# Two small loads on GpSimd's queue, tiles ahead of a weight, no zero products, and a new table of ranks in a gated spectral and dense mix

## The chip, the cores and the metric

The kernel runs on one core of a Trainium2 chip. Its engines each run a program of their own in order: TensorE (PE) multiplies, VectorE (DVE) and ScalarE (ACT) work element by element, GpSimd (POOL) and SyncE (SP) here mostly issue DMAs; ACT issues three. The metric is the device time of one execution in microseconds, and less is better. Times come from several runs; the profile comes from one further, recorded execution.

## The reference, cut to what matters

```python
def reference(A_x, A_w_r, A_w_i, B_x, B_w1, B_b1, B_w2, B_b2, gate_w):   # x: 1 x 2048 x 512
    x = A_x
    g = sigmoid((x * gate_w).sum(-1, keepdims=True))
    a = irfft2(rfft2(x) * (A_w_r + 1j * A_w_i))          # weights 2048 x 257
    b = gelu(x @ B_w1 + B_b1) @ B_w2 + B_b2              # 512 -> 1792 -> 512
    return g * a + (1 - g) * b
```

The input x is A_x in both branches. All is float32.

## The kernel before, in words

The 2048 tokens are 16 tiles j of 128; tile j of x has its 512 features on partitions, in four quarters. Tile class c is j mod 4, so class 0 holds the tiles 0, 4, 8, 12. A product in full precision is made of three products in a faster format (fp32r): each operand is split into a high part (h, by ACT) and a low part (l, by DVE: the rest), and hh, hl and lh are summed in PSUM. So `mxh`, `mxl` are the parts of x, `wa0h`, `wa0l` those of the first block of B_w1 (14 blocks f of 128 columns), `wb0h`, `wb0l` of B_w2, `g0_6h`, `g0_6l` those of the gelu output of class 0, block 6.

The spectral branch goes through `forward` for each tile (sums and differences of the quarters `eo` and `w`, a transform over the features into `pd`, one over the tokens of the tile into `py`, result `y`), then radix-4 steps between tiles on DVE (`stage1`, `filt`, `stage4`, tiles named a0, b1, c0 and so on; `filt` multiplies by the filter `wf`), then `inverse` (`pz`, `pa`). The gate's weights (`gw`, in the tile `g3`) are combined by five tiny DVE operations and put as two columns into the constant `cf` of the feature transform, so that the logits fall out of `pd`.

The dense branch has two halves. For the classes 0 and 1, `mlp` makes for each block f a group `ph` of 12 products of 512 columns, ACT applies bias (`b1t`) and gelu, the result is split, and `down` sums groups `po` over the blocks. The first group, class 0 and block 0, starts tile by tile: its products have 128 or 256 columns, since only tiles 0 and 4 are there at first. For the classes 2 and 3, `fast` makes two blocks of weights against two classes of tokens with seven products instead of eight: it uses sums of inputs (`xf11`, `xft1` and so on), of weights (`wa0h0`, `wash0`, `wath0`), two groups `nu` and two banks `ux0`, `ux1` that live through the whole half. A bank of `ux` receives by an ACT copy a result already made, and products are then added on top without the flag that starts a group. Before the first use both banks are set by one product each with a zero tile (`zerob`, lines 1168 to 1171).

PSUM has eight banks in two groups; of the class `ph` at most two are open, so a third group `ph` waits until the low part of the one two before has been read out by DVE.

What sets the order: the code adds about 2000 steps to a graph, each with an engine, a cost and a lag, and what it reads and writes. The table `RANKS` holds one number for each step, in the order in which the code adds them; a low number goes first. `schedule` plays the engines with costs and lags and takes on each engine the ready step with the lowest rank; that gives each engine's order, which is fixed at run time. A queue's DMAs are issued in that order too, each as soon as its semaphore and its tile are free. On the chip an engine that waits holds up all behind it.

The lines that the steps touch: x tiles are loaded by `load_x` (line 569); tiles 0 (by ACT's queue) and 4 by lines 594 and 596; gate weights by line 600; `cf` by 602; the bias by 625; weights by `load_w` (981 for block 0, 984 for others, 968 for those that a copy makes negative). POOL issues the DMAs that add while they write (line 498), and clears some columns of `zb` at the start (607).

## Time and profile before

| | us |
|---|---|
| median of 3 runs (365.37 to 367.65) | 365.63 |
| the profiled execution | 368.04 |
| its span, first to last instruction | 366.2 |
| PE busy | 358.7 |
| DVE busy | 327.8 |
| ACT busy | 256.7 |
| POOL busy | 69.6 |

The profiled execution's time lies 1.84 us above its span. In a row of the timeline stand start, duration, engine, line, operation, output and inputs, how many in a row, and in brackets the idle time ahead of it with what ended it. PE rows overlap: a product's duration is longer than the distance to the next. In a row of the waits stand who waited for whom, then the sum in us, the number of times and the longest. In a row of the DMA view, the last number is the median from issue to landing. In a row of the windows, behind the stretch and its length, stand the busy times of PE, of its weight loads, of DVE, ACT and POOL, then the granted clock, the share of the DMA engines and GB/s. A digit of the page's second part is a tenth of busy time.

### The profile page before, as it was taken

Reading aid. Unit: us, or ns where it says so; the run is one execution under the profiler, and the core shown is the slowest. Engines: PE = TensorE matmul, PEld = TensorE weight load, DVE = VectorE, ACT = ScalarE, POOL = GpSimd, SP = SyncE. Lnnn points to the kernel's source line nnn. Section 1 sums busy time; section 2 is a strip of 40 time slices with the busy share of each in tenths; the row PEclk is TensorE's granted clock in tenths of the full one; section 3 lists DMA queues with packets and bytes.
Section 4 is the critical chain, followed back from the end, with each engine's and each line's share of the span. In section 5 each row is a group of like instructions: output and inputs, shape, how many; then the busy total and the mean of one; then the engine's idle time right before and its main releaser. Section 6 shows DMA issues by size and latency. Waiting matters only on the chain.

```text
span 366.2 us, 5746 instructions
## 1 busy us (share of the span) xinstructions
PE 358.7 (98%) x1808; PEld 302.9 (83%) x1808; DVE 327.8 (90%) x746; ACT 256.7 (70%) x471; POOL 69.6 (19%) x89
## 2 busy tenths in 40 slices
PE   8999999999999999999999999999999999999994
PEld 8888898898878778878888788888888888888884
DVE  5999988998759999899999999999999769899962
ACT  4985778789986241753759975999999998655200
POOL 0210001100211311410333100002333112121220
PEclk9999999999999999999999999999999999999999
DMA  7999785647885937999999943339887637799896
GB/s 224 306 322 303 253 233 166 106 149 233 206 204 129 189 58 155 273 263 365 196 153 217 264 85 117 86 122 225 126 141 150 100 64 156 173 296 241 199 250 184
DMA packets 46719, 70.35 MB, mean 192 GB/s; under 512 B 5600, under 2 KB 19424, under 8 KB 46688
## 3 DMA queue, kind: packets, MB, share of 16 engines
q1 hardware_dynamic: 34880, 48.93, 41.8%
q0 software_dynamic: 11376, 20.71, 35.3%
q10 hardware_dynamic: 432, 0.33, 0.3%
q8 instruction: 14, 0.23, 0.3%
q14 instruction: 17, 0.14, 0.1%
HBM read 48.32 MB, written 19.41 MB: 185 GB/s over the span
## 4 chain that ended last, share of the span: by engine, by line
PE 75%; DVE 12%; DMA 5%; ACT 4%; issue 2%; SPq 1%; DVEq 0%; ACTq 0%
PE poB L507 20%; PE po L507 13%; PE ph L507 11%; PE ux L1185 9%; PE nu L1185 7%; PE pd L507 4%; PE pz L507 3%; PE py L507 3%; PE pa L507 3%; DVE m L856 3%; DMA wf<-in_wf 3%; DMA y<-ownr 1%; DMA xf<-in_xt 1%; DVE y L760 1%; DVE y L758 1%
## 5 line engine op out<-in xcount | busy, mean ns | idle before, releaser
L995 ACT ACTIVATE ph<-ph,b1t 128x512 f32<-128x512 f32 x28 | 18.4, 658 | 25.5 <-PE ph L507 25.2
L498 POOL DMA_DIRECT2D bacc<-o x16 | 15.3, 1029 | 43.2 <-ACT o L1073 43.2
L894 ACT ACTIVATE sw<-y,al 64x512 f32<-64x512 f32 x32 | 22.8, 718 | 0.6
L498 POOL DMA_DIRECT2D bacc<-oB x16 | 13.9, 889 | 43.0 <-ACT oB L1073 33.7
L856 DVE TENSOR_TENSOR m<-y,wf 128x514 f32<-128x514 f32 x32 | 20.7, 688 | 0.0
L507 PE MATMUL pd<-cf,w 128*128 128x129 f32 x128 | 17.7, 276 | 0.0
L507 PEld LDWEIGHTS pz<-tg,pq 128*128 128x128 f32 x128 | 16.8, 191 | 1.1
L507 PEld LDWEIGHTS pd<-cf,w 128*128 128x128 f32 x128 | 16.6, 191 | 1.2 <-DVE zb L698 0.3
L1185 PE MATMUL nu<-xf,wa0h 128*128 128x512 f32 x56 | 17.3, 390 | 0.0
L507 PE MATMUL pz<-tg,pq 128*128 128x128 f32 x128 | 17.2, 274 | 0.0
L507 PE MATMUL py<-zb,tf 128*128 128x258 f32 x96 | 17.1, 295 | 0.0
L723 ACT ACTIVATE y<-pys 64x257 f32<-64x257 f32 x32 | 13.2, 417 | 3.9 <-DVE pys L720 3.4
L507 PE MATMUL pa<-zb,ci 128*128 128x256 f32 x96 | 15.2, 285 | 0.2 <-ACT od L935 0.2
L507 PEld LDWEIGHTS pa<-zb,ci 128*128 128x128 f32 x96 | 13.8, 189 | 1.9 <-ACT od L935 0.7
L507 PEld LDWEIGHTS py<-zb,tf 128*128 128x128 f32 x96 | 14.1, 190 | 1.2 <-ACT pys L716 0.2
L1073 ACT ACTIVATE o<-po 128x512 f32<-128x512 f32 x16 | 9.2, 593 | 8.3 <-PE po L507 8.2
L901 DVE SCALAR_TENSOR_TENSOR pq<-y,al,sw 128x256 f32<-128x256 f32 x32 | 14.4, 479 | 0.0
L695 ACT ACTIVATE zb<-pd 128x256 fp32r<-128x256 f32 x32 | 11.6, 384 | 3.9 <-PE py L507 3.9
L698 DVE TENSOR_TENSOR zb<-pd,zb 128x256 fp32r<-128x256 f32 x32 | 12.5, 417 | 1.1 <-ACT zb L695 1.1
L665 DVE TENSOR_TENSOR w<-eo 128x256 f32<-128x256 f32 x32 | 12.8, 418 | 0.0
L662 DVE TENSOR_TENSOR eo<-xf 128x256 f32<-128x256 f32 x32 | 12.4, 419 | 0.0
L1185 PEld LDWEIGHTS nu<-xf,wa0h 128*128 128x128 f32 x56 | 10.5, 188 | 2.2
(701 smaller groups left out, 1274.3 us busy)
## 6 DMA issues: line engine op xcount, KB each, us to landing
wf<-in_wf SPq DMA_DIRECT2D x16, 257.0 KB, 4.7
bacc<-o POOLq DMA_DIRECT2D x16, 256.0 KB, 6.1
bacc<-oB POOLq DMA_DIRECT2D x16, 256.0 KB, 4.9
xf<-in_xt SPq DMA_DIRECT2D x14, 256.0 KB, 5.0
wr<-in_w SPq DMA_DIRECT2D x14, 256.0 KB, 4.9
tf<-tf SPq DMA_DIRECT2D x16, 192.0 KB, 2.8
bacc<-o SPq DMA_DIRECT2D x8, 256.0 KB, 3.2
ba<-bacc SPq DMA_DIRECT2D x8, 256.0 KB, 4.1
```

The lines of the kernel that those rows point to most:

```text
L498: return add("pool", 2.3 * kb / 340, 3.4, lambda: nc.gpsimd.dma_start(dst(), src(), accum_op=ALU.add), reads, writes, rank)
L507: pe.matmul(ps, w, x, start=start, stop=stop)
L662: v(lambda s=s, op=op: vec.tensor_tensor(eo.ap()[:, s], x.ap()[:, 0:2], x.ap()[:, 2:4], op=op), 256, [x], [(eo, s)], feed)
L665: v(lambda s=s, op=op: vec.tensor_tensor(w.ap()[:, s], eo.ap()[:, :, 0], eo.ap()[:, :, 1], op=op), 256, [eo], [(w, s)], feed)
L695: a(lambda c=c: act.activation(segs(xh, c), both(c), AF.Copy), 256, [ps[c]], [(xh, c)], 0)
L698: v(lambda c=c: vec.tensor_tensor(segs(xl, c), both(c), segs(xh, c), op=ALU.subtract), 256, [ps[c], (xh, c)], [(xl, c)], 0)
L723: a(lambda o=o, i=i: act.activation(Y[j].ap()[o:o + HP, 1], pys.ap()[i:i + HP, 1], AF.Copy), 257, [(pys, 1)], [(Y[j], 1 + k)], 0, more=0.1)
L856: v(lambda mk=mk, k=k, y=y, w=w: vec.tensor_tensor(mk.ap(), y.ap(), w.ap()[:, k:k + 1, :ND].to_broadcast([P, 2, ND]), op=ALU.mult), 514, [ ...
L894: a(lambda sw=sw, y=y, o=o, i=i: act.activation(sw.ap()[o:o + HP], y.ap()[i:i + HP, ::-1, :HD], AF.Copy, scale=al.ap()[i:i + HP, 0:1]), 51 ...
L901: v(lambda sw=sw, pq_=pq_, y=y, j=j, k=k, op=op: vec.scalar_tensor_tensor(pq_.ap()[:, k], y.ap()[:, k, :HD], al.ap()[:, 1 + j:2 + j], sw.a ...
L995: a(lambda: act.activation(ps.ap(), ps.ap(), AF.Gelu_apprx_tanh, bias=b1t.ap()[:, f:f + 1]), 600, [b1t], [ps]).table = "gelu"
L1185: pe.matmul(o.ap(), w(wi, e), FX[j].ap()[:, xi, e], start=first, stop=k == 5, skip_group_check=not start)
```

## The change

Four edits in the code, and a new table:

- the gate weights and the first bias are loaded by POOL's queue, no longer SP's;
- the zero tile and the two products that set the banks `ux` are gone; the ACT copy is the first that touches the banks in the second half;
- lags of the first loads are other numbers for the scheduler (they cost nothing on the chip, but they change the order);
- `RANKS` is new throughout, so the order on all engines is new.

```diff
 RANKS = """
-0 12 294 321 326 399 330 333 323 340 343 1 13 7 14 20 23 11 35 26 10 2 5 8 19 4 32 56 47 53 78 22 42 73 43 45 21 25 72
+7 4 6 24 26 29 33 13 37 16 25 2 15 0 17 18 23 11 19 36 8 5 139 1 9 14 47 138 87 72 83 45 22 79 73 21 30 35 109 100 103
...
-        dma(lambda: sp.dma_start(x.ap(), xt[j]), 256, [], [x], j / 100 if j in NORD[:4] else turn_of(NORD.index(j) - 2))
+        add("sp", 256 / 340, 1.4 if j in NORD[:4] else 2.8, lambda: sp.dma_start(x.ap(), xt[j]), [], [x],
+            j / 100 if j in NORD[:4] else turn_of(NORD.index(j) - 2))
...
-        dma_act(lambda k=k: act.dma_start(x0.ap()[:, 2 * k:2 * k + 2].rearrange("p a b -> p (a b)"),
-                                          x0g[:, k * HD:(k + 1) * HD]), 128, [], [(x0, k)])
-        add("sp", 128 / 340, 2.4, lambda k=k: sp.dma_start(x4.ap()[:, 2 * k:2 * k + 2], xt[4][:, 2 * k:2 * k + 2]), [], [(x4, k)],
+        add("act", 0.4, 2.45, lambda k=k: act.dma_start(x0.ap()[:, 2 * k:2 * k + 2].rearrange("p a b -> p (a b)"),
+                                                        x0g[:, k * HD:(k + 1) * HD]), [], [(x0, k)], 0)
+        add("sp", 128 / 340, 1.0, lambda k=k: sp.dma_start(x4.ap()[:, 2 * k:2 * k + 2], xt[4][:, 2 * k:2 * k + 2]), [], [(x4, k)],
...
-    dma(lambda: sp.dma_start(gw.ap().rearrange("p a b -> p (a b)"), x0g[:, NQ * P:]), 8, [], [gw], 0.5)
+    add("pool", 0.1, 3.5, lambda: nc.gpsimd.dma_start(gw.ap().rearrange("p a b -> p (a b)"), x0g[:, NQ * P:]), [], [gw], 0)
...
-        dma(lambda c=c: sp.dma_start(cft.ap()[:, c], cf_d[c]), 129, [], [(cft, k) for k in (c, 2 + c)], 0.6)
+        add("sp", 129 / 340, 1.8, lambda c=c: sp.dma_start(cft.ap()[:, c], cf_d[c]), [], [(cft, k) for k in (c, 2 + c)], 0.6)
...
-        dma(lambda: sp.dma_start(b1t.ap(), b1), 7, [], [b1t], 0.45)
+        add("pool", 0.1, 4.0, lambda: nc.gpsimd.dma_start(b1t.ap(), b1), [], [b1t], 0.1)
...
-                add("sp", 128 / 340, 1.9 + 0.3 * k, lambda o=o: sp.dma_start(t.ap()[:, o], src[:, o]), [], [(t, k)])
+                add("sp", 128 / 340, 1.0 + 0.2 * k, lambda o=o: sp.dma_start(t.ap()[:, o], src[:, o]), [], [(t, k)])
...
-            dma(lambda: sp.dma_start(t.ap(), src), 256, [], [t])
+            add("sp", 256 / 340, 1.2 if f == 1 else 2.8, lambda: sp.dma_start(t.ap(), src), [], [t])
...
-            zero = buf("w", [P, P], F32R, "zerob", cls="zero")
-            add("vec", 0.3, 0.1, lambda: vec.memset(zero.ap().bitcast(F32), 0.0), [free[CA[1]]], [zero])
-            for x in free["X"]:
-                m(lambda x=x: mm(x.ap(), zero.ap(), bcast(zero.ap(), 4), True, True), 512, 1, [zero], [x])
```

Three places in the order follow. In the names the number behind the last underscore tells the buffer and means nothing here; `war1` is the raw weight block 1, `xf8` tile 8.

The start of SP's queue before (all DMAs):

```order
L981 DMA war0_80<-in_w1 128x256 x2
L600 DMA g3_99<-in_x0g 128x4
L596 DMA xf4_101<-in_xt 128x256 x2
L984 DMA war1_104<-in_w1 128x512
L968 DMA wb0l_raw_106<-in_w2 128x512
L625 DMA b1t_112<-in_b1 128x14
L569 DMA xf8_120<-in_xt 128x512
L569 DMA xf12_128<-in_xt 128x512
L602 DMA cf_137<-cf 128x258
```

And the start of SP's queue now:

```order
L982 DMA war0_82<-in_w1 128x256 x2
L597 DMA xf4_103<-in_xt 128x256 x2
L569 DMA xf8_106<-in_xt 128x512
L603 DMA cf_108<-cf 128x258
L569 DMA xf12_116<-in_xt 128x512
L985 DMA war1_122<-in_w1 128x512
L603 DMA cf_108<-cf 128x258
L969 DMA wb0l_raw_134<-in_w2 128x512
```

The tiles 8 and 12 have moved ahead of weight 1, and the gate weights (g3) and the bias (b1t) have left the queue. On POOL the bias now stands behind one clearing of `zb`, then five more, then the gate weights, then the adding DMAs as before.

DVE's queue around the first operation on the gate weights (g3), before:

```order
L651 TENSOR_TENSOR mxl00_134<-xf4_101,mxh00_114 128x512
L614 TENSOR_TENSOR g3_99<-g3_99 128x2
L987 TENSOR_TENSOR wa0l_151<-war0_80,wa0h_109 128x512
L662 TENSOR_TENSOR eo4_162<-xf4_101 128x256
L987 TENSOR_TENSOR wa1l_164<-war1_104,wa1h_146 128x512
```

And now:

```order
L652 TENSOR_TENSOR mxl00_129<-xf4_103,mxh00_114 128x512
L663 TENSOR_TENSOR eo0_112<-xf0_76 128x256
L615 TENSOR_TENSOR g3_101<-g3_101 128x2
L988 TENSOR_TENSOR wa0l_150<-war0_82,wa0h_110 128x512
L663 TENSOR_TENSOR eo4_159<-xf4_103 128x256
L663 TENSOR_TENSOR eo8_163<-xf8_106 128x256
L663 TENSOR_TENSOR eo12_171<-xf12_116 128x256
L652 TENSOR_TENSOR mxl00_129<-xf12_116,mxh00_114 128x512
L988 TENSOR_TENSOR wa1l_182<-war1_122,wa1h_161 128x512
```

The gate operation still stands right ahead of wa0l; work on the tiles 8 and 12 has moved ahead of wa1l. On PE, the four products of tiles 8 and 12 with wa0h now come ahead of every product with weight 1. From the first product with weight 1 on, 32 products of 256 columns make up the rest of the first two groups; before, 24 were left from the first product with tiles 8 and 12 on.

PE at the start of the second half, before (from the first zero product on):

```order
L507 MATMUL ux1_2303<-zerob_2295 128x512
L507 MATMUL po2_13_2291<-g1_12h_2191,wb12h_1923 128x512
...
L1185 MATMUL nu00_2314<-xf11_334,wa0l0_2231 128x512
L507 MATMUL po2_12_2267<-g1_13h_2210,wb13h_1935 128x512
...
L507 MATMUL ux0_2334<-zerob_2295 128x512
L507 MATMUL po2_13_2291<-g1_13h_2210,wb13h_1935 128x512
...
L1185 MATMUL nu01_2346<-xft1_359,wash0_2244 128x512 x2
...
L1185 MATMUL ux0_2334<-xft2_460,wash0_2244 128x512 x2
```

And now:

```order
L1182 MATMUL nu00_2312<-xf11_368,wa0l0_2229 128x512
L507 MATMUL po2_13_2289<-g1_12h_2185,wb12h_1903 128x512
L507 MATMUL po2_13_2289<-g1_12l_2198,wb12h_1903 128x512
L507 MATMUL po2_13_2289<-g1_12h_2185,wb12l_1941 128x512
L507 MATMUL po2_13_2289<-g1_13h_2200,wb13h_1935 128x512
L507 MATMUL po2_13_2289<-g1_13l_2216,wb13h_1935 128x512
L507 MATMUL po2_13_2289<-g1_13h_2200,wb13l_1945 128x512
L1182 MATMUL ux0_2336<-xft2_436,wash0_2242 128x512 x2
```

Both zero products are gone; the first product that adds on the copied nu00 in ux0 stands six products behind the end of nu00, and the group nu01, which stood ahead of it before, follows it.

DVE around g1_6l, the low part of class 1's block 6, whose reading frees the bank for the group ph1_8, before:

```order
L760 SCALAR_TENSOR_TENSOR b1u1_1616<-y_536 128x257
L858 TENSOR_TENSOR y_536<-m1_12_1599,m2_12_1603 128x257
L756 TENSOR_TENSOR b1u2_1623<-y_536 128x257
L860 TENSOR_TENSOR y_536<-m1_12_1599,m2_12_1603 128x257
L558 TENSOR_TENSOR g1_6l_1631<-ph1_6_1476,g1_6h_1625 128x512
L851 SCALAR_TENSOR_TENSOR wf5_1583<-wf5_1583,rev_166 128x2x2
L864 TENSOR_TENSOR y_536<-y_536 128x8
```

And now:

```order
L852 SCALAR_TENSOR_TENSOR wf1_1559<-wf1_1559,rev_303 128x2x2
L865 TENSOR_TENSOR y_536<-y_536 128x8
L761 SCALAR_TENSOR_TENSOR b1u1_1624<-y_536 128x257
L759 TENSOR_TENSOR c0d0_1626<-y_536 128x2x256
L759 TENSOR_TENSOR c0d1_1633<-y_536 128x2x256
L558 TENSOR_TENSOR g1_6l_1638<-ph1_6_1483,g1_6h_1631 128x512
L757 TENSOR_TENSOR c0s0_1645<-y_536 128x2x256
```

Two operations c0d now stand ahead of g1_6l. On PE three products (po1_03 with g0_8) have moved ahead of ph1_8.

PE at the group ph1_12, which waits for the bank of ph1_10 (freed by g1_10l), before:

```order
L507 MATMUL ph1_11_2012<-mxh01_326,wa11l_1543 128x512
L507 MATMUL po2_01_2047<-g0_10h_1747,wb10h_1868 128x512
L507 MATMUL po2_01_2047<-g0_10l_1819,wb10h_1868 128x512
L507 MATMUL po2_01_2047<-g0_10h_1747,wb10l_1885 128x512
L507 MATMUL ph1_12_2056<-mxh01_326,wa12h_1563 128x512
```

And now:

```order
L507 MATMUL ph1_11_2013<-mxh01_301,wa11l_1561 128x512
L507 MATMUL ph1_12_2047<-mxh01_301,wa12h_1555 128x512
L507 MATMUL ph1_12_2047<-mxl01_365,wa12h_1555 128x512
L507 MATMUL ph1_12_2047<-mxh01_301,wa12l_1568 128x512
```

The three products po2_01 that stood between the two groups have moved behind ph1_12.

154 rows, old and new, of the table RANKS are left out of this document.

## Prediction

> **What bounds the kernel now.** I read the page's first part first, then the waits of TensorE, then the busy time between its first steady product and its last, then one long row of the chain.
>
> ```profile
> span 366.2 us, 5746 instructions
> PE 358.7 (98%) x1808; PEld 302.9 (83%) x1808; DVE 327.8 (90%) x746; ACT 256.7 (70%) x471; POOL 69.6 (19%) x89
> ```
> ```profile
> 13.48:361.49 348.01, 346.88 (x1744) 292.06 (x1742) 318.57 (x720) 248.55 (x457) 67.22 (x77) 1.00 0.78 190
> ```
> ```profile
> PE ph L507 <- ACT mxh L650: 0.6, 1, 0.6
> PE ph L507 <- DVE g_10l L558: 0.5, 1, 0.5
> PE ph L507 <- DVE g_6l L558: 0.3, 1, 0.3
> PE pa L507 <- ACT od L935: 0.2, 1, 0.2
> ```
> ```profile
> 174.48 14.30 PE po L507 x63
> ```
>
> In the long stretch TensorE (PE) is busy for 346.88 of 348.01 us, at granted clock 1.00. The chain's row gives the pitch of its commonest work: 63 products of 512 columns in 14.30 us, 0.227 us each. So PE itself is the bound, and an edit can win only what stands ahead of 13.48, the four named waits (1.6 us together), the tail behind 361.49, and products that are taken out. VectorE (DVE) at 90% is the second bound: where the order makes PE wait for it, time is lost. Everything here is small beside 366.
>
> The sum is made against the profiled execution: span 366.2, 368.04 in all, so 1.84 lies around the span. The runs' median is 365.63, 2.41 under that execution; I put the change of the span onto the median.
>
> **Step 1: the two zero products.** Before, two banks (ux) were set to zero by a product each.
>
> ```profile
> 188.61 0.39 PE L507 MATMUL ux<-zerob 128*128 128x512 f32 x1
> 188.84 0.39 PE L507 MATMUL po<-g_12h,wb12h 128*128 128x512 f32 x1
> ...
> 191.56 0.39 PE L507 MATMUL ux<-zerob 128*128 128x512 f32 x1
> ```
> ```profile
> 191.99 0.58 ACT L1191 ACTIVATE ux<-nu 128x512 f32<-128x512 f32 x1 [0.89 <-PE ux L507]
> ```
>
> Each costs its pitch, 188.84 - 188.61 = 0.23 us, on an engine that never rests there: -0.45. ScalarE (ACT) also stood 0.89 us behind the second one before it copied into the bank. In the new order the reader of that copy comes right after six products (6 x 0.227 = 1.36 us of cover) where six more lay between before. The copy takes 0.58 and its source is ready when the six begin, so it is covered, unless ACT is late by more than 1.36 - 0.58 = 0.8 us; then the 0.45 is given back, so this step lies between 0 and -0.45. I take -0.45, since ACT stood idle just there. The memset for the zero tile on DVE goes too, and I count it as nothing.
>
> **Step 2: the start.** What ends last at the start are the token tiles 8 and 12.
>
> ```profile
> 4.99 4.81 DMA xf<-in_xt
> ```
> ```profile
> 3.06 0.43 SPq L984 DMA_DIRECT2D war<-in_w  x1
> ...
> 4.51 0.91 SPq L569 DMA_DIRECT2D xf<-in_xt  x2
> ...
> 6.46 0.63 ACT L985 ACTIVATE wa1h<-war 128x512 fp32r<-128x512 f32 x1 [0.24 <-DMA war<-in_w]
> ...
> 9.10 1.35 ACT L650 ACTIVATE mxh<-xf 128x512 fp32r<-128x512 f32 x2 [1.36 <-DMA xf<-in_xt]
> ...
> 10.50 0.74 PE L507 MATMUL ph<-mxh,wa1h 128*128 128x256 f32 x4 [0.64 <-ACT mxh L650]
> ...
> 13.48 1.95 PE L507 MATMUL pd<-cf,w 128*128 128x129 f32 x16
> ```
> ```profile
> war<-in_w SPq DMA_DIRECT2D x5, 256.0 KB, 5.4
> ```
>
> Before, PE stops until tile 12 is copied, starts at 10.50, and needs 2.98 us for the 24 products that are left (0.124 each). The issues on SyncE's queue (SP) stand 0.47 us apart (4.51 to 4.99). In the new order tile 12 is the sixth DMA there instead of the ninth: its issue moves from 4.99 to about 3.54, its landing from 9.8 to about 8.3. But weight 1 moves from 3.06 to about 4.04, behind both tiles, and behind it 32 products are left, not 24. It landed 3.4 us after its issue before (6.46 against 3.06) and its group's median is 5.4. So it lands between 7.4 and 9.4; I take tile 12's 4.81, since that transfer stood behind as many others: 8.85. Its copy of 0.63 ends at 9.5, and 32 x 0.12 = 3.9 us later, with the last of it as dense as before, PE is at 13.3 or 13.4 instead of 13.48: -0.1 to -0.25. With the early landing, tile 12's copies bound it instead, about 12.7 (-0.8); with the late one 14.0 (+0.5). I take -0.25, for the two small transfers that leave SP's queue also take 0.9 us of issue time from it. The tiles win little because the stop is handed to the weight. No later issue on SP is made dearer by that: what stands behind weight 1 now was behind the two tiles before.
>
> **Step 3: gate weights and bias on GpSimd's queue (POOL).**
>
> ```profile
> 0.74 0.26 POOL L607 MEMSET zb<- 128x2 f32 x6 [0.29 <-POOLq L1360]
> ...
> 3.31 0.29 DVE L982 CAST wa0h<-war 128x256 fp32r<-128x256 f32 x1 [2.31 <-DMA war<-in_w]
> ...
> 6.87 0.15 DVE L614 TENSOR_TENSOR g<-g 128x2 f32<-128x2 f32 x1
> ...
> 6.94 0.68 DVE L987 TENSOR_TENSOR wa0l<-war,wa0h 128x512 fp32r<-128x512 f32 x1
> ...
> 7.54 0.42 DVE L662 TENSOR_TENSOR eo<-xf 128x256 f32<-128x256 f32 x1
> ...
> 11.29 1.01 POOL L498 DMA_DIRECT2D wb0l<-in_w  x1 [10.30 <-DMA rev<-in_wrev]
> ...
> 13.77 0.64 ACT L995 ACTIVATE ph<-ph,b1t 128x512 f32<-128x512 f32 x1
> ```
> ```profile
> g<-in_x0g SPq DMA_DIRECT2D x1, 2.0 KB, 2.7
> ```
> ```profile
> wb0l<-in_w POOLq DMA_DIRECT2D x1, 256.0 KB, 7.2
> ```
>
> POOL is idle for 10.30 us there, so two issues of about 1.0 (the 11.29 row) hold up nothing on it: the bias is issued at about 0.8, the gate weights, behind it and the memsets, at about 1.9. The bias is read at 13.77, far behind any landing. The gate weights are wanted by DVE at about 6.9, and the low part of weight 0 is queued right behind that little operation. How long a small transfer by POOL takes no row shows: the same 2 KB by SP took 2.7, POOL's first large one 7.2, so it lands between 4.6 and 9.1. I take 4.6, since the size is that of the first row, and with it the step costs nothing. The cover ends when the gate operation starts after 7.5: behind it come wa0l 0.68, three sums of 0.42 and another 0.68 until wa1l, which wants weight 1's copy (9.5) anyway.
>
> **Step 4: the order.** Two of the named waits are waits for a free bank: PE may start a new group (ph) only when DVE has taken the low part of the one two before it.
>
> ```profile
> 123.36 0.68 DVE L558 TENSOR_TENSOR g_6l<-ph,g_6h 128x512 fp32r<-128x512 f32 x1
> 124.52 0.17 DVE L851 SCALAR_TENSOR_TENSOR wf<-wf,rev 128x4 f32<-128x4 f32 x1 [0.47 <-DMA wf<-in_wf]
> ...
> 124.80 1.29 DVE L758 TENSOR_TENSOR c0d<-y 128x512 f32<-128x512 f32 x2
> ```
> ```profile
> 124.10 0.50 PE L507 MATMUL ph<-mxh,wa8h 128*128 128x512 f32 x1 [0.35 <-DVE g_6l L558]
> ```
> ```profile
> 163.93 0.68 DVE L558 TENSOR_TENSOR g_10l<-ph,g_10h 128x512 fp32r<-128x512 f32 x1
> ```
> ```profile
> 164.66 0.50 PE L507 MATMUL ph<-mxh,wa12h 128*128 128x512 f32 x1 [0.51 <-DVE g_10l L558]
> ```
>
> At 124.10 three products more now stand ahead of the waiting group (0.68 of cover), but g_6l now stands behind the two c0d operations (1.29), which leave out an idle of 0.47. So the wait of 0.35 changes by between -0.35 (gone) and 1.29 - 0.68 = +0.6. At 164.66 the three products that were cover (0.68) now follow the group, and g_10l has moved up by about one operation of 0.6: between -0.5 and +0.7. The two together I take at +0.2, near the middle, since each pays one way and wins the other. In the rest of the second half moves of some us either way stand on all engines, with PE's own work the same but for the zero products.
>
> **Tail.**
>
> ```profile
> 361.21 0.28 PE L507 MATMUL poB<-g_13h,wb13lb 128*128 128x256 f32 x1
> ...
> 361.52 0.42 DVE L1266 TENSOR_TENSOR oB<-y,poB 128x256 f32<-128x256 f32 x1 [0.23 <-PE poB L507]
> 361.97 0.33 SPq L1269 DMA_DIRECT2D out<-oB  x1
> ```
>
> The last half block's single subtraction and DMA change places with the half that is cut in two small ones on two queues: within 0.1 either way, taken as 0.
>
> **Sum:** -0.45 - 0.25 + 0 + 0.2 + 0 = -0.5. The span would be 365.7 and the time 365.63 - 0.5 = 365.1 us, -0.14%. About 1% (3.7 us) is what a measurement of this kernel can tell from no change, so this is no change by that measure.
>
> **The rivals.**
>
> - *The gate weights land late (slower).* If POOL's small transfer takes 7.2 us, DVE holds wa0l until 9.1. Then wa0l 0.68, three sums 1.26, a low part 0.68 and wa1l 0.68 end at 12.4, and 24 products (2.9) behind it end at 15.3: 1.8 later than 13.48, 2.05 above my start. 365.1 + 2.05 = 367.2. It decides from 7.5 on, 5.6 us after the issue. For it: POOL's 7.2 was met with all DMA engines loaded, as here. Against it: 2 KB, not 256. The Trainium skill ("SBUF — State Buffer", section "SBUF: two separate sides") warns that GpSimd can't write descriptors while VectorE holds the port they share. The rows above have DVE idle for 2.31 us until 3.31, with the issue at 1.9 in that gap, so I give that rule no more than this rival's share. The Trainium skill ("DMA: Bandwidth & Descriptors", section "Anatomy of one DMA — SWDGE (gpsimd) path") fits 2.0 us and a little for such a transfer; by that the sum is as it stands.
> - *The new order makes new bank waits (slower).* If the 0.6 of g_6l comes true in three places, as there are three such named waits in the long stretch, +1.8 instead of +0.2: 366.7. For it: DVE at 90%, and its rows have moved by several us. Against it: PE has as many products to put between.
> - *The new order closes the waits (faster).* If both bank waits (0.35 + 0.51) and pa's 0.2 go, and weight 1 lands early (-0.8): -0.45 - 0.8 - 1.06 = -2.3, 363.3. For it: the order was made with other landing times for the first tiles. Against it: at 164.66 the cover was taken away.
>
> **How the numbers follow.** My forecast, 364.2 to 366.2: 0.52. Late gate weights, 367.2: 0.10. New waits, 366.7: 0.18. Waits closed, 363.3: 0.20. The range takes in the low ends together (-0.45 - 0.8 - 0.85, and a tail of -0.1, with pa's 0.2: 363.2) and the high ends without the late gate weights (0 + 0.5 + 1.8: 367.9), cut to hold 8 in 10: 363.0 to 367.7. To be faster by over 1% (under 362.0) more than all that is named would have to go: 0.05, out of the last case. Slower by over 1% (over 369.3) needs late gate weights and new waits together: 0.07. The rest, 0.88, is within 1%.
>
> **What would show it.** Step 1: no ux<-zerob rows, and no wait of PE ahead of its first ux product. Step 2: ACT waits for war, not xf, ahead of the second group, and pd starts at 13.2 to 13.4. Step 3: no idle of DVE ahead of the first g operation; an idle there, ended by a DMA, is the first rival. Step 4: PE's waits for g_6l and g_10l in the waits view, still there with about 1 us together. Wrong would be a sum of PE's named waits far from 1.6, or pd before 12.7 or after 14.

## The result, and the profile after

The changed kernel takes 367.94 us (median of 22 runs, 366.99 to 371.37), the kernel before 366.88 beside it (22 runs): ratio 1.0045, 95% interval 1.0028 to 1.0061. By the ratio it is slower by 0.45%, 1.65 us of 366.9; the quotient of the two medians is less, 1.0029 (1.06 us). Single executions over 1.5% above the fastest of their kernel (374.22 of the kernel before here; 369.41, 372.21 and 613.03 in the experiments) count in the medians and not in the ratios. The profiled execution took 369.03 us, span 367.3.

The page's first part, and TensorE's (PE's) long stretch in the view by windows, from the first steady product to the last (columns: window, its length, then busy time and count of PE, weight loads, VectorE (DVE), ScalarE (ACT) and GpSimd (POOL), the granted clock, DMA share, GB/s):

```profile
span 367.3 us, 5751 instructions
PE 359.8 (98%) x1806; PEld 303.2 (83%) x1806; DVE 328.9 (90%) x745; ACT 256.9 (70%) x471; POOL 70.3 (19%) x91
```
```profile
15.09:363.89 348.80, 346.71 (x1742) 291.44 (x1740) 317.99 (x713) 248.41 (x456) 66.36 (x77) 1.00 0.78 188
```

The long stretch begins at 15.09 instead of 13.48 and is 0.79 us longer with two products less: both the start and the steady part got worse in this execution. PE's waits are other ones:

```profile
PE none L507 <- DVE zero L576: 1.1, 1, 1.1
PE poB L507 <- DMA wb4lb<-in_w: 0.9, 1, 0.9
PE nu L1182 <- DVE zb L915: 0.6, 1, 0.6
PE poB L507 <- DMA wb5lb<-in_w: 0.4, 1, 0.4
PE ph L507 <- ACT mxh L651: 0.3, 1, 0.3
PE ph L507 <- DVE mxl L652: 0.3, 1, 0.3
PE ph L507 <- DVE wa0l L988: 0.3, 1, 0.3
```

The waits for g_6l and g_10l, on which the prediction's fourth step rested, are gone, and so is the one for od. In their place PE waits in the second half for the low parts of weights 4 and 5 (wb4lb, wb5lb), which POOL completes by an adding DMA, and for a bank that DVE frees (zb).

The start, on ACT and PE, in the timeline (start, length, what it is; in brackets the idle time before it and what ended it):

```profile
8.63 0.63 ACT L651 ACTIVATE mxh<-xf 128x512 fp32r<-128x512 f32 x1 [1.29 <-DMA xf<-in_xt]
9.26 0.63 ACT L986 ACTIVATE wa1h<-war 128x512 fp32r<-128x512 f32 x1
```
```profile
7.26 0.74 PE L507 MATMUL ph<-mxl,wa0h 128*128 128x256 f32 x4 [0.29 <-DVE mxl L652]
8.27 0.74 PE L507 MATMUL ph<-mxh,wa0l 128*128 128x256 f32 x4 [0.26 <-DVE wa0l L988]
9.32 1.22 PE L507 MATMUL ph<-mxh,wa0h 128*128 128x256 f32 x4 [0.30 <-ACT mxh L651]
10.34 1.05 PE L507 MATMUL ph<-mxh,wa1h 128*128 128x256 f32 x4
11.19 1.05 PE L507 MATMUL ph<-mxl,wa1h 128*128 128x256 f32 x4
12.04 0.81 PE L507 MATMUL ph<-mxh,wa1l 128*128 128x256 f32 x4
...
14.61 0.64 PE L507 MATMUL ph<-mxh,wa0l 128*128 128x256 f32 x4
15.09 1.17 PE L507 MATMUL pd<-cf,w 128*128 128x129 f32 x9
```
```profile
9.00:12.40 3.40, 3.10 (x15) 3.08 (x15) 3.33 (x10) 2.95 (x6) 0.53 (x1) 0.50 1.00 324
```

PE has three small gaps from 7.0 to 9.3. From 9.0 to 12.4 the granted clock is 0.50, so four products of 256 columns take 0.85 us (10.34 to 11.19) where they take 0.48 at 14.61. The Trainium skill ("TensorE: Matmul & The Clock Gate", "Part 1: The HAM clock gate") has windows of 3413 ns, half rate after an idle one and full rate after a busy one; the trace agrees on the length, one stretch of 3.41 us, but the 3.41 us ahead of it were not idle: PE was busy for 2.73 of them. How little work is enough to lose the full clock no run here shows.

The profiled execution is not the common case. A stretch of 3.41 us at half rate lowers the mean granted clock of an execution to 0.995, and 7 of the 22 runs of the changed kernel have that mean; the other fifteen have 0.999 or more. (Where in the run the stretch lies is recorded for the profiled one alone.) The median of the seven is 368.63 us, that of the fifteen 367.67. So the stretch goes with about 1 us more in a run that has it, but with only 0.3 in the median of all 22: it is not the main part of the slowdown. Whether the half rate or the late data ahead of it costs this 1 us, these runs can't tell.

The gate weights, now on POOL's queue, are no obstacle: issued at 2.19, 3.4 us to landing, used at 7.46 with no idle time of DVE ahead of it.

```profile
2.19 0.58 POOL L601 DMA_DIRECT2D g<-in_x0g  x1
```
```profile
7.46 0.15 DVE L615 TENSOR_TENSOR g<-g 128x2 f32<-128x2 f32 x1
```
```profile
g<-in_x0g POOLq DMA_DIRECT2D x1, 2.0 KB, 3.4
```

**Lost time.** To compare places I use one measure below: PE's lost time at an instant is that instant less the pitch of all work that PE has begun by then in the kernel's own order (0.227 us for 512 columns, 0.111 for a pd or pz pass, and so on). All the work is 348.72 us before, 348.27 without the two zero products. Worked out from every PE row of each trace:

| profiled execution | its time | 15.2 us | 30 | 190 | 350 |
|---|---|---|---|---|---|
| before | 368.04 | 5.74 | 6.09 | 10.39 | 12.46 |
| after | 369.03 | 7.33 | 7.45 | 9.59 | 15.26 |

By these two traces the start loses 1.4 more at 30 us, the middle (30 to 190) wins 2.2, and the late part (190 to 350) loses 3.6. One trace of each is thin evidence for such sums: the profiled execution of before lay 1.2 over its median. So the pieces were run by themselves.

### The profile page after: what moved, and what is told of

Read it like the earlier page. It is cut to its first block, busy times and chain, and to the rows that moved or that the text cites. A ratio compares the mean times of both kernels' runs of the same rounds, so it can differ in the third digit from the quotient of the medians.

```text
span 367.3 us, 5751 instructions
## 1 busy us (share of the span) xinstructions
PE 359.8 (98%) x1806; PEld 303.2 (83%) x1806; DVE 328.9 (90%) x745; ACT 256.9 (70%) x471; POOL 70.3 (19%) x91
## 4 chain that ended last, share of the span: by engine, by line
PE 82%; ACT 6%; DMA 5%; DVE 4%; issue 1%; DVEq 0%; POOLq 0%
PE ph L507 21%; PE po L507 21%; PE poB L507 16%; PE ux L1182 7%; PE nu L1182 6%; PE pd L507 4%; PE py L507 3%; PE pz L507 2%; DMA wb5lb<-in_w 2%; PE pa L507 2%; DMA xf<-in_xt 1%; DMA bb<-bacc 1%; ACT sw L895 1%; DMA xf<-in_x0g 1%; DVE zb L915 1%
## 5 line engine op out<-in xcount | busy, mean ns | idle before, releaser
L498 POOL DMA_DIRECT2D bacc<-o x16 | 15.2, 996 | 42.7 <-ACT o L1074 42.7
L498 POOL DMA_DIRECT2D bacc<-oB x16 | 14.7, 949 | 42.1 <-ACT oB L1074 42.1
L507 PE MATMUL py<-zb,tf 128*128 128x258 f32 x96 | 18.2, 296 | 0.0
L507 PE MATMUL pa<-zb,ci 128*128 128x256 f32 x96 | 14.3, 282 | 0.0
L936 ACT ACTIVATE od<-pa 128x512 f32<-128x512 f32 x8 | 4.8, 597 | 10.8 <-DVE oB L1263 6.6
```

Of the source, the lines that this page charges most:

```text
L498: return add("pool", 2.3 * kb / 340, 3.4, lambda: nc.gpsimd.dma_start(dst(), src(), accum_op=ALU.add), reads, writes, rank)
L507: pe.matmul(ps, w, x, start=start, stop=stop)
```

## The experiments

Most of these kernels take the order of the steps from one kernel up to some instant and from the other behind it. The order is written out as a list, and the buffers' places are dealt out anew by the same rule (first free, first taken); nothing else differs from the changed kernel:

```diff
-    order = g.schedule()
+    order, places = [g.steps[int(n)] for n in ORDER.split()], iter(PLACES.split())
+    for s in order:
+        for b in s.bufs:
+            if b.slot is None:
+                b.slot = int(next(places))
```

**First cuts.** Four such lists: changed order to 200 us, then before's; before's to 195 us, then the changed; before's start of 16 us; and a mixture.

> The changed kernel up to about 200 us; all that is left then is issued in the order of the kernel before (no zero products). By the time that TensorE loses (its start times less the pitch of its work) the new order loses 1.6 us more before the first pd product (7.33 against 5.74), 2.4 less from there to 190 (2.26 against 4.65), and 3.6 more behind (5.73 against 2.14), and its tail is some 1.2 shorter. Theory (each stretch keeps its own cost): 366.9 + 1.6 - 2.4 - 0.45 = 365.6 us, about 2.3 under the changed kernel's 367.9, and no wait for wb4lb and wb5lb. Rival (the late waits are the price of what was won in the middle, work that is only put off): they come back in this order too, 367 to 368.

Measured: 366.35 (before 366.21; ratio 1.0000, 0.9976 to 1.0024).

> The kernel before up to about 195 us (its zero products left out, gate weights and first bias by GpSimd's queue as in the changed kernel), and behind it what is left in the changed kernel's order, its tail too. Theory (each stretch keeps its own cost): 366.9 - 0.45 + 3.6 - 1.2 = 368.8 us, with TensorE waiting for wb4lb and wb5lb. Rival (the late waits are put-off work of the middle): 366.9 - 0.45 - 1.2 = 365.2, without these waits.

Measured: 370.91 (1.0125, 1.0093 to 1.0158).

> The first 16 us in the order of the kernel before (weight 1 ahead of tiles 8 and 12 on SyncE's queue, first half of tile 0 first on ScalarE's), but gate weights and bias still by GpSimd's queue; all behind it in the changed kernel's order. Theory (the start's order costs 1.6): 367.9 - 1.6 = 366.3 us, pd at 13.5 or sooner, granted clock 1.0 there. Rival (the small transfers by GpSimd's queue hold up the start): pd stays at about 15, 367.9.

Measured: 370.11 (1.0110, 1.0087 to 1.0133), though 4.56 us were lost at 15.2 instead of 7.33.

> The order of the kernel before for the first 16 us, the changed kernel's from there to about 200 us, the order before from there to about 350 us, and the changed kernel's tail; no zero products, gate weights by GpSimd's queue. Theory (each stretch keeps its own cost): 366.9 - 0.45 - 2.4 - 1.2 = 362.8 us, under both kernels. Rival (the gain of the middle is paid back behind it): 365.2.

Measured: 369.06 (1.0080, 1.0051 to 1.0109).

Neither theory gave these. The lost time jumps at the seams: from 4.56 at 15.2 us to 8.59 at 30 where the cut was at 16, and from 7.37 at 200 to 11.93 at 210 where it was at 195. There one order counts on work that the other has still to do. A wait of the third kernel, behind its seam (the place where the order changes from one to the other):

```profile
PE ph L507 <- DVE wa3l L988: 3.7, 1, 3.7
```

These four say little about the change. The next cuts stand where both orders have nearly the same work behind them: at 36, 42, 180, 300 and 305 us.

**The parts one by one.** The zero products alone, taken out of the kernel before:

```diff
         for s in order:
-            s.emit()
+            if all(b.name != "zerob" for b in s.bufs):
+                s.emit()
```

> The kernel before without the two zero products and the zero tile's memset; nothing else is changed. Theory (they cost their pitch on TensorE, and ScalarE's copy behind them is covered): 0.45 under the kernel before (366.2 on this chip's last runs, so 365.8). Rival (given back by a wait for that copy): 0, within 0.1 of the kernel before.

Measured: 366.42 against 366.28 (1.0000, 0.9981 to 1.0020). The forecast's -0.45 (0.9988) lies inside that interval, so the run can't tell it from 0.

The two small transfers alone, in the kernel before:

```diff
-    dma(lambda: sp.dma_start(gw.ap().rearrange("p a b -> p (a b)"), x0g[:, NQ * P:]), 8, [], [gw], 0.5)
+    dma(lambda: nc.gpsimd.dma_start(gw.ap().rearrange("p a b -> p (a b)"), x0g[:, NQ * P:]), 8, [], [gw], 0.5)
...
-        dma(lambda: sp.dma_start(b1t.ap(), b1), 7, [], [b1t], 0.45)
+        dma(lambda: nc.gpsimd.dma_start(b1t.ap(), b1), 7, [], [b1t], 0.45)
```

> The kernel before with one change: the gate weights and the first bias are issued by GpSimd's queue instead of SyncE's; the order and the zero products stay. Theory (it takes 0.9 us of issue time from SyncE's queue at the start, and TensorE begins about 1.0 sooner): 1.0 to 1.2 under the kernel before, 365.2 of 366.3. Rival (that gain belonged to the zero products that were taken out with it): within 0.4 of the kernel before.

Measured: 364.10 against 366.39 (0.9939, 0.9923 to 0.9955): 2.3 us faster, from two DMA issues, and twice what was expected. In its trace PE's waits at the start are gone and pd begins at 12.15 instead of 13.48:

```profile
11.67 0.64 PE L507 MATMUL ph<-mxh,wa1l 128*128 128x256 f32 x4
12.15 1.06 PE L507 MATMUL pd<-cf,w 128*128 128x129 f32 x8
```
```profile
3.54 0.90 SPq L569 DMA_DIRECT2D xf<-in_xt  x2
```

Tiles 8 and 12 are issued 0.97 us sooner than before (3.54 against 4.51). The two transfers were moved together, so what each is worth was not tried.

The same without the zero products, in the order of before (the base for what follows):

> The order of the kernel before, without the zero products, and with the gate weights and the first bias issued by GpSimd's queue at their old places in the order. Against the kernel before without zero products it shows the two small transfers alone. Theory (they cost nothing on either queue): the same, about 365.8. Rival one (SyncE's queue gains 0.9 us at the start, and the tiles land so much earlier): about 1.0 less, 364.8, with 4.5 us lost ahead of the first pd, as in the kernel that begins in the order of before, against 5.74. Rival two (gate weights late): more than 366.2.

Measured: 364.69 (0.9967, 0.9943 to 0.9991). Rival one gave it. Against the kernel before without zero products (366.42, measured beside it) the two transfers are worth 1.2 us by the ratios and 1.7 by the medians here, less than the 2.3 above; pd begins at 13.01 in this trace, at 13.21 without the move.

The changed order's start, its middle, and its late part, each with the order before elsewhere:

> The changed kernel's order up to 42 us, then that of the kernel before, cut where both have the same work behind them; no zero products, gate weights and bias by GpSimd's queue. To be held against the same kernel with the order before throughout (364.7). Theory (the start with tiles 8 and 12 ahead of weight 1 is dearer): lost time at 40 us of 6.8 to 7.5 against 4.8 to 5.6, so 1.3 to 2 more: 366.0 to 366.7. Rival (the order up to 180 us is dearer for its middle, not its start): 364.7.

Measured: 366.75 (1.0017, 0.9999 to 1.0035), 2.1 over the base.

> The order before up to 36 us, the changed kernel's from there to 180 us, the order before behind it; no zero products, gate weights and bias by GpSimd's queue. Theory (the middle of the new order loses 2.1 to 2.5 between 30 and 190 us against 2.8 to 3.3, the waits for g_6l, g_10l and a bank are gone): 0.6 to 0.9 less than the same kernel with the order before throughout, 363.8 to 364.1, under both kernels. Rival (no gain): 364.7 or more.

Measured: 363.87 (0.9930, 0.9907 to 0.9953), 0.8 under the base and 0.7% under the kernel before. That is as fast as the kernel before with the two transfers moved and nothing else (364.10): these two can't be told apart.

> The order of the kernel before up to 180 us (no zero products, gate weights and bias by GpSimd's queue), behind it that of the changed kernel, cut at a place where both have the same work behind them. Theory (the loss lies behind 180 us): 3.6 more there and 1.2 less in the tail than the same start with the order before behind it: 367.2 to 368.2, with waits for wb4lb and wb5lb and at 327. Rival (put-off work of the middle): at most 365.3, without them.

Measured: 366.85 (1.0021, 0.9993 to 1.0050), 2.2 over the base. Two of PE's waits there:

```profile
PE nu L1182 <- DVE zb L915: 0.9, 1, 0.9
...
PE poB L507 <- DMA wb5lb<-in_w: 0.4, 1, 0.4
```

> The changed kernel's order up to 180 us, then that of the kernel before, cut at a place where both orders have the same work behind them (the cuts at 16 and 200 us left TensorE with a wait at the seam of 1.4 to 4.5 us). Theory (the loss of the changed kernel lies behind 180 us): the changed order loses 8.9 us up to there without the slow stretch of the clock, the order before 2.1 behind it: 11.0, with 348.27 of work 1.95 less than in the kernel before's profile, and some 0.5 to 1.9 less than its median: 364.3 to 365.7. Rival (the late waits are put-off work of the middle): 366.5 to 368, with waits for wb4lb and wb5lb.

Measured: 366.04 (0.9993, 0.9973 to 1.0014), without a wait for wb4lb or wb5lb; the base with the start (+2.1) and the middle (-0.8) would be 366.0.

The theory (each stretch keeps its own cost, once the cut is clean) fits: from 366.3 to 364.7 by the two transfers and the zero products, then +2.1 for the start's order, -0.8 for the middle, +2.2 for the late part: 368.2, where the changed kernel has 367.9. Each of these differences is uncertain by 1.0 to 1.4 us. By the ratios, which hold each kernel against before in the same session, the start is +1.8 and, between the kernel with the changed order up to 180 us and the one with the middle alone, +2.3. The late part is +2.0 and, between the changed kernel and the one changed up to 180 us, +1.9. The middle is -1.4 and, between the kernels changed up to 180 and up to 42 us, -0.9. So the costs of the start and of the late part are each shown twice, and the gain of the middle is at the edge of what the runs can show. The traces back it: all ten with the changed order in the middle lose less between 30 and 190 us than any of the ten with the order before (the profile after 2.1 us by the table above, its nine fellows up to 0.5 more, the others 0.7 to 2.2 more).

**The small transfers in the changed order.** Both issued by SyncE's queue again, behind weight 0 and behind wb0l.

```diff
-    add("pool", 0.1, 3.5, lambda: nc.gpsimd.dma_start(gw...
+    add("pool", 0.1, 3.5, lambda: sp.dma_start(gw...
-        add("pool", 0.1, 4.0, lambda: nc.gpsimd.dma_start(b1t...
+        add("pool", 0.1, 4.0, lambda: sp.dma_start(b1t...
```

> The changed kernel with the gate weights and the first bias issued by SyncE's queue again, at about their old places (behind weight 0, and behind wb0l). Theory (the two small transfers cost the start the same in any order): 1.5 to 2.2 more than the changed kernel's 367.9, 369.4 to 370.1. Rival (in the new order they hold up less, since weight 1 comes late anyway): 0 to 0.5 more, 367.9 to 368.4.

Measured: 369.60 (1.0094, 1.0069 to 1.0119) where the changed kernel has 1.0045: 1.8 us more. So that part of the change is worth about 2 us in either order.

**Why the start's order is dear.** Three edits of the kernel with the changed start (366.75). The first puts more zero products into PE's gaps:

```diff
+    warmer = {517: 3, 518: 4, 519: 4}
...
         for s in order:
+            for _ in range(warmer.get(s.n, 0)):
+                mm(none.ap()[:, :2], zero.ap(), bcast(zero.ap(), 2), True, True)
             s.emit()
```

> The kernel with the changed start (up to 42 us) and the order before behind it, 366.75 us, with eleven more products of the zero tile in the three gaps that TensorE has between 7.0 and 9.3 us; their result is read by nobody. Theory (the idle pieces bring the half clock from 9.0 to 12.4 us, which costs 1 us): the granted clock is 1.0 there, pd starts at 13.0 to 14.1 instead of 15.1, and the time is some 0.5 to 1.0 less, 365.7 to 366.2. Rival (the start is late by its data, the clock is covered later): 366.75 as before, or more by the products that don't fit (up to 0.5).

Measured: 367.44 (1.0035, 1.0008 to 1.0061). The clock did what the theory said, in its trace and in all 12 runs (mean granted clock 0.998 or more):

```profile
9.00:12.40 3.40, 3.40 (x31) 3.40 (x30) 3.37 (x13) 2.94 (x6) 1.02 (x2) 1.00 1.06 345
```

and pd began at 13.21, but the time did not get shorter. It could hardly do so: only 2 of the 12 runs of the kernel with the changed start have the half clock (0.994 and 0.995, the profiled one among them), and the median of the other ten is 366.5. So the half clock is not the price of 2.1 that the median shows, and what it costs a run that has it this experiment can't say.

The second loads tile 0 and weight 0 first half first:

```diff
 SyncE, ScalarE and VectorE, in the order of issue
-war0[second half], war0[first half]; xf0[second half], xf0[first half]
+war0[first half], war0[second half]; xf0[first half], xf0[second half]
-wa0h, eo0, wa0h, mxh
+wa0h, wa0h, mxh, eo0
```

> The same kernel (changed start, order before behind 42 us, 366.75 us), with tile 0 and weight 0 loaded first half first, as before the change, and VectorE's casts ahead of its first sum. Theory (the first product waited 0.87 us for the half that came second): the first mxh of ScalarE at 3.5 instead of 4.3 to 4.5, and 0.5 to 0.9 less, 365.9 to 366.2. Rival (tile 4's low part and wa0l set the pace behind it): the first product is earlier, pd is not, 366.75.

Measured: 366.46 (1.0010, 0.9993 to 1.0027). ACT's first copy moved from 4.52 to 3.59, but pd stood at 13.49, where two traces of the changed start with a full clock have 12.97 and 13.11. The rival holds: 0.3 less, which is within the uncertainty.

The third puts weight 1 ahead of the tiles again:

```diff
 SyncE
 war0 x2, xf4 x2
-xf8, cf, xf12, war1, cf
+war1, xf8, cf, xf12, cf
 TensorE
-(ph0) mxh8,12 x wa0h; (ph1) mxh x wa1h, mxl x wa1h, mxh x wa1l
+(ph1) mxh x wa1h, mxl x wa1h, mxh x wa1l; (ph0) mxh8,12 x wa0h
```

> The kernel with the changed start (up to 42 us) and the order before behind it, 366.75 us, with weight 1 ahead of tiles 8 and 12 again: its load on SyncE's queue, its copy on ScalarE, its low part on VectorE, and its first twelve products on TensorE ahead of those of tiles 8 and 12. Theory (the tiles ahead of the weight are the price of the start): 1.3 to 2 less, 364.7 to 365.4, pd at 12.2 to 13.0. Rival (the price lies in the order of the other engines' steps of the first 42 us): 366.2 or more.

Measured: 366.50 (1.0007, 0.9993 to 1.0021). pd began at 12.80. That is 2.3 us sooner than in the trace of the kernel it was edited from, but that trace is one of the two with the half clock; against this start at full clock (12.97 and 13.11) it is 0.2 to 0.3, and the time stayed. More is lost behind pd: this trace has lost 5.07 us at 15.2, and 6.88 at 30. The kernel whose start is the changed kernel's and whose clock stayed full (changed order up to 180 us) shows the same, 5.37 and 7.07, and where:

```profile
26.63 0.40 PE L507 MATMUL po<-g_1h,wb1l 128*128 128x512 f32 x1
27.82 0.59 PE L507 MATMUL py<-zb,tf 128*128 128x258 f32 x3 [0.79 <-DMA tf<-tf]
```

PE waits for the first table (tf). The changed order issues it at 13.9 to 15.2 in its traces, and its tables take 7.6 to 13.3 us to landing; the order before with the two transfers moved issues it at 10.2 to 11.1, with 5.3 to 5.6 to landing (the kernel before at 11.81, with 5.3):

```profile
14.41 1.15 SPq L504 DMA_DIRECT2D tf<-tf  x1
```
```profile
10.91 0.43 SPq L504 DMA_DIRECT2D tf<-tf  x1
```

(The first row is of the kernel just named, the second of the base.) The start of the changed order has two bounds, one behind the other: the first products, and then this table at 27 to 28 us. Where the first is late, as in the profile after, the second does not show. The wait for the table stands in four traces with a full clock (0.3 to 1.0 us), but not in those of the two edits before, which were no faster by their runs. The two traces of this start that are not edited and have the full clock have lost 2.0 us more at 40 us than six traces with the start before (by means; the two transfers on POOL in all). Of that, 0.6 is there at 15.2 us, and 1.3 comes behind it, where these two wait 0.8 and 0.5 for the table. So the table explains a part at most; what else makes up the 2.1 stays open, and a kernel with the table alone moved was not tried.

**Why the late part is dear.** Two places of the changed kernel mended:

```diff
 ScalarE, at 248 us
+wb5hb<-wb5lb_raw, wb5lb<-wb5hb
 oB<-poB,b
 nu<-nu,b1t
-wb5hb<-wb5lb_raw
 sw<-y,al
-wb5lb<-wb5hb
 VectorE, at 327 us
-u<-pa,od
 zb<-pz,zb
+u<-pa,od
```

> The changed kernel with two places behind 240 us mended: ScalarE makes weight 5's high and low parts ahead of an oB and a nu step instead of behind them, and VectorE takes the low part of zb ahead of a sum (u) at 327 us. Theory (each named wait is the price): the wait for wb5lb (0.4, with what stands around it 0.56) and the wait of nu for zb (0.6, with what stands around it 0.72) go, 1.0 to 1.3 less than the changed kernel, 366.6 to 366.9. Rival (ScalarE and VectorE are full there, and another wait takes the place): no more than 0.4 less, 367.5 or more.

Measured: 368.82 (1.0065, 1.0038 to 1.0092), nothing won. The wait for wb5lb is gone, and so is the one for wb4lb (its transfer took 5.4 us to landing, not 6.7), but right behind the same products stands a new one, for ACT:

```profile
257.81 0.39 PE L507 MATMUL poB<-g_5h,wb5lb 128*128 128x512 f32 x1
259.33 0.98 PE L507 MATMUL pa<-zb,ci 128*128 128x256 f32 x6 [1.13 <-ACT od L936]
```

ACT makes od at 258.68 here and at 258.58 in the profile after: it comes no sooner, and PE, which is 1.2 us ahead at these products (256.65 for their first, 257.89 in the profile after), waits for it. The wait for zb stayed at 0.7 although DVE takes the low part of zb ahead of the sum:

```profile
325.21 0.69 DVE L1232 SCALAR_TENSOR_TENSOR bb<-gb,bb 128x512 f32<-128x512 f32 x1 [1.81 <-DMA bb<-bacc]
...
327.08 0.69 DVE L915 TENSOR_TENSOR zb<-pz,zb 128x512 fp32r<-128x512 f32 x1
```
```profile
325.02 1.09 ACT L914 ACTIVATE zb<-pz 128x512 fp32r<-128x512 f32 x2
```

The high part, on ACT, is ready at 326.11. DVE comes to the low part a microsecond later, since it stood 1.81 us for a load (bb, the dense branch's sum that is read back) and then worked without a pause. That idle, 1.1 to 2.0 us, stands ahead of this zb in all six traces in which PE waits for it, and in the profile before it is 0.17. So the two waits that were mended were not what bound PE there: ACT's queue and the load of bb stood right behind them. The rival holds: a mended wait turns into another.

The late part cut in two:

> The order before up to 36 us, the changed kernel's from there to 300 us, the order before behind it; no zero products, gate weights and bias by GpSimd's queue. To be held against the same kernel with the cut at 180 us, 363.9. Theory (of the 2.2 us lost behind 180, the waits for wb4lb and wb5lb and what stands around them are 0.9 to 1.2, the wait of nu for zb at 327 us and what stands around it 1.0 to 1.3): 364.8 to 365.1. Rival one (all of it lies at 327): 363.9. Rival two (all of it lies ahead of 300): 366.1.

Measured: 365.77 (0.9988, 0.9964 to 1.0012), 1.9 over the kernel with the cut at 180.

> The order before up to 36 us, the changed kernel's to 180 us, the order before to 305 us, the changed kernel's behind it; no zero products, gate weights and bias by GpSimd's queue. To be held against the same kernel with the order before behind 180 us (363.9) and against the one with the changed order to 300 us (365.8). Theory (the wait of nu for zb at 327 us and what stands around it is 1.0 to 1.3): 364.9 to 365.2, with that wait there. Rival (nearly all of the late loss lies ahead of 300, as the runs with the cut at 300 have it): 363.9 to 364.2.

Measured: 363.85 (0.9936, 0.9919 to 0.9953), as the kernel with the cut at 180, although its trace has the wait for zb (1.0). That trace is of its slowest run (366.48, with a half clock at the start); whether the other five, at 362.97 to 364.81, have the wait isn't recorded.

By the runs nearly all of the 2.2 lies ahead of 300 us; by the traces 1.1 lies there (lost time at 350 us 11.04 against 9.93) and 1.3 at 320 to 330. Each of the runs' differences has an uncertainty of about 1 us, and how the loss divides stays open.

## Why the prediction was wrong

It said 365.1 us, within 363.0 to 367.7, faster by 0.14%. It is 367.9 and 0.45% slower: the sign is wrong, and the range is missed by 0.2 us. Of the 2.8 us between, 1.25 is that the kernel before has 366.88 beside the change, where the first three runs gave 365.63; 1.6 is the sum's: -0.5 was forecast, and 1.06 more is measured by the medians. That the change is within 1% was right. That a measurement can't tell less than 1% was not: the interval here is 0.33% wide.

- **Step 1 (zero products, -0.45): right in kind, the size not settled.** The rows are gone and the work is 0.45 us less. The copy into the bank ends at 204.25 (203.67 + 0.58) and the product behind it begins at 204.31, 0.28 after the one ahead of it at 204.03 instead of 0.23; so the cover was just enough. By runs the part is 0, give or take 0.7.
- **Step 2 (start, -0.25) and step 3 (gate weights by POOL, 0): the two sizes were wrong and nearly cancel, by luck.** Step 3 was right that the gate weights are not late, but it was not worth 0: it won 2.3 and 1.2 us in the old order (two pairs of kernels) and 1.8 in the new. I had put the 0.9 us of freed issue time into step 2 and there let weight 1 eat it up. Step 2 had its landings nearly right (weight 1's copy began at 9.26, where I took 8.85 and 9.4 at most for the landing; tile 12's at 8.63, said 8.3), but "32 x 0.12 = 3.9 us later, with the last of it as dense as before" failed in the profiled execution: some ten of the 32 products ran at half clock, the work took 4.75 us, and pd began at 15.09, behind the 14 that was named as a sign of being wrong. In most runs the clock stayed full, and with it this start has pd at 12.97 and 13.11, near the forecast 13.3. What failed for those is that the step looked only as far as pd and against the wrong start: with the two transfers moved, the order before has pd at 12.0 to 13.0 at full clock, and the table tf, which the new order issues 3 to 4 us later, was not in the sum at all. By runs the start's order costs 2.1, of which these traces explain a part. "No later issue on SP is made dearer by that" was misread, too: wb0l stood ahead of the tiles 8 and 12 before and stands behind weight 1 now, and the table failed it. (Tile 12 is the seventh DMA there instead of the tenth, not the sixth instead of the ninth; the three places between are right.)
- **Step 4 (order, +0.2): the named waits were mis-sized, and the rest was left out.** The waits for g_6l and g_10l, which I left at about 1 us together, are gone, and the middle is worth -0.8, give or take 1.2. But for the second half I wrote that moves of some us stand on all engines "with PE's own work the same", and counted 0. It costs 2.2: PE's own work is the same, but it waits for wb4lb, wb5lb and zb, and behind these for ACT's od and for DVE, which stands for bb. This is the term that turned the sign; which of these waits sets how much of it stays open.
- **Tail (0): right.** From the start of PE's last product to the end of the span are 3.65 us after, and 3.60 to 3.95 in the eighteen traces of the experiments. The 5.04 in the trace of before was that execution's own.

Of the rivals, late gate weights did not happen. "The new order makes new bank waits" (0.18, 366.7) came nearest in kind (in time the 367.2 of late gate weights is nearer, by chance), but I had placed it in the middle, at waits like those of g_6l; it came behind 190 us, at weights' low parts and at zb. "The new order closes the waits" was right for the middle alone, as far as the runs can show its gain. The middle and the late part are one order, made as one; I judged it by the two places where before had waits, and a place without a wait before was not looked at.

## What to carry to other kernels

When a schedule is made anew, the places to price are those where the old one had little slack, not those where it waited: for each transfer that is issued later, find its first reader. A wait that is mended shows the next one: ask first when the engine behind it will be ready, and what that engine itself waits for. Two traces can differ by what one of them happened to do: look at the clock of all runs before a profiled execution is taken for the common case. And it is worth trying to keep small loads off the queue that brings the first operands: two of the smallest transfers of this kernel were the ones worth moving, and alone they make it 0.6% faster. The middle of the new order on top of that (0.7%) can't be told from it.

## What the runs showed of the hardware that was not expected

- Two transfers of 2 and 7 KB cost 2.3 us on the queue of the first tiles (1.2 and 1.8 by two other pairs of kernels), though an issue is only 0.47 us there. In this pair of traces 1.3 of it is seen at pd. DMA traffic in the first 14 us, before and with the two on POOL's queue (the GB/s row has 40 slices of 0.35 us):

```profile
GB/s 0 0 0 0 0 129 161 319 345 375 222 167 187 258 366 375 392 402 273 288 263 252 259 240 293 255 243 328 366 385 383 384 399 404 340 369 357 357 316 287
DMA packets 3038, 3.76 MB, mean 268 GB/s; under 512 B 713, under 2 KB 1737, under 8 KB 3038
```
```profile
GB/s 0 0 0 0 0 88 208 378 313 372 338 275 348 400 351 357 304 263 334 310 349 352 354 408 348 378 386 370 383 400 375 386 380 334 316 222 269 322 310 322
DMA packets 2982, 4.06 MB, mean 290 GB/s; under 512 B 509, under 2 KB 1533, under 8 KB 2982
```

  From 3.5 to 4.6 us the rate falls to 167 to 222 GB/s before, and stays at 275 to 348 with the two moved, which have 204 packets fewer under 512 B. The Trainium skill ("DMA: Bandwidth & Descriptors", "Specifications") wants 512 B for full rate, which fits. But such a valley stands in the trace of the changed start too (155 to 207), with the transfers on POOL, and its cause there is open.
- In the profile after, PE was busy for 2.73 of 3.41 us and had the half clock for the next 3.41. By their mean clock, 7 of the 22 runs of this kernel had such a stretch and fifteen had none. The seven are about 1 us longer (368.63 against 367.67); 3.41 us at half rate would by itself be worth 1.7.
- The same adding DMA of 256 KB (wb4lb) took 6.7 us to landing in the profile after and 4.5 before, and 6.4 and 5.5 in two other traces of the changed late order; PE's wait for it comes and goes with that (0.9 us, 0.5 and none).
- Two profiled executions of one order (but for the zero products) differ by 1.5 us of lost time at 190 us (10.39, and 8.91 without the zero products), as much as the whole change: traces show where, and only runs how much.
